# A new order of all operations in a hand-scheduled adaLN, SSM-convolution and gMLP kernel, with four groups of filler matmuls instead of six

## The chip, the core and the metric

The kernel runs on one core of a Trainium2 chip. The metric is the device time in microseconds (us) of that core, the median of several runs. The profile names the engines PE (TensorE matmuls; PEld is its weight load), DVE (VectorE), ACT (ScalarE), POOL (GpSimd) and SP (SyncE, which here only issues DMA transfers).

## What is computed

One transformer-like block on a sequence of 2048 rows of 640 columns, all in bf16, with a condition `c` that gives six row vectors.

```python
mod = silu(c) @ w_mod                                   # six vectors sa, ca, ga, sb, cb, gb of 640
h = layernorm(q) * (1 + ca) + sa
kv = short_conv(k, shift_k) * v                         # four taps along the sequence
y  = irfft(rfft(kv, 2S) * rfft(ssm_k, 2S))[:S] + kv * ssm_D     # long convolution by FFT
x  = q + ga * (h * y)
h = layernorm(x) * (1 + cb) + sb
z = gelu(h @ w_in);  z1, z2 = halves of 864;  z2 = layernorm(z2)
g = w_sp @ z2 + b_sp                                    # w_sp is 2048 x 2048
out = x + gb * ((z1 * g) @ w_out)
```

## The kernel before

**Operations and their order.** The kernel first builds a list of 1438 operations (`Plan.op`). An operation is a small closure that issues one or more instructions: `taps` is 64 matmuls, `csum` one tensor-tensor step, `ldwo` seven DMA transfers. Each has a number, a kind, the letters of the engines that may run it, and the operations that it depends on. Nothing is then decided at run time: the string `ORDER` lists all of them once, each as a letter for its engine (P TensorE, A ScalarE, D VectorE, G GpSimd, S the DMA queue of SyncE) and its number, and `Plan.run` issues them in that order. An engine works through its own tokens one after the other; an instruction that waits for another engine or a transfer holds up all that stand behind it on its engine. So `ORDER` fixes both which engine does a step and what stands in front of what in each queue.

**The convolution** (the first 145 us or so) runs in five units of 128 columns, `u` = 0 to 4. For each, the taps of the short convolution are matmuls against diagonal matrices (`taps`), VectorE multiplies them with `v` (`tv`), a transposing DMA regroups the result (`kvt`, L625), and a first transform stage of matmuls (`s1`, evicted by `s1c`, L272) feeds the second: eight `fwd` matmul groups for the filter (evicted by `khc`) and eight for the signal, whose products are taken on VectorE (`prod`, L489), summed on GpSimd or VectorE (`csum`, L503), transformed back on TensorE (`inv`) and evicted (`zc`). The result is transposed by a DMA (`zt`) or, for the last unit, on TensorE (`zfl`), and multiplied into `gh`, the normalized and modulated input (`ln1`, `xn`, `ghm` at L727). The tables of cosines that all this uses are made at the start on VectorE, GpSimd and ScalarE (`turns` L370, `msub`, `msin`, `msgn`, `mneg`, `gcopy`, `gneg`), and the column `D` is widened (`dwide`), turned and added to the filter (`addD`, L427). `res` adds the branch to `x`.

**The fillers** are matmuls of the identity with itself, 512 columns each, into a PSUM tile that nobody reads. `FILLS` gives the number in each group; the profile shows them as `s<-ident`.

**The gate's input** (about 130 to 205 us) runs in four groups of 512 rows. Statistics (`ln2`, `ag2`, `rstd2`, `nmr2`), normalization (`zx`), a turn into column order (group 0 by TensorE, `hfl`, L928; groups 1 to 3 by a transposing DMA, `turn`, L959), modulation (`hmod`, or `hmod2` at L967, five per group), 16 matmul groups `zz` with GELU behind each, statistics (`stz`, `agz`) and normalization (`zn`) of the second half.

**The mixing and the last product** (from about 180 us) form the 2048 x 2048 product and the output projection by Strassen-like schemes. For each of eight pairs `p` of row blocks, two transposed loads of `w_sp` (`wT`, L1044), four sums (`ssum`, L1057), and seven products `prodw`; VectorE and GpSimd join them with the bias `bcol` and with `z1` into `u` (`c11`, `partial`, `c22a`, `c22b`, `c22m`, `lsa`, and the product step `lsm`, L1115), a transposing DMA turns `u` (`turnu`), sums are formed (`usum`, in the function `u_sum`), and eight products of 320 columns (`pq`, L1291) or the plain form (`pp`, L1304) are joined with `x` (`os`, `oa`, `ox`, `pa`) and stored. `w_out` is loaded by seven transfers (`ldwo`, L1154) and multiplied by `gb` in place (`gbm`, L1159).

Of the kernel before, what the change touches and what calls it, by code (L numbers as in the profile page):

```python
# [33 lines left out]
FILLS = (4, 6, 2, 2, 4, 3, )  # L34
# [9 lines left out]
G5 D13 D101 D0 D14 A1 G102 S525 D103 S2 D116 D15 P7 A10 S23 D104 S83 S84 S26 G122 D117 G6 A4 P1034 A38 S24 D18 A532 P8  # L44
D128 D123 A11 A118 G25 A119 S27 A16 P39 D17 D20 D87 D110 S3 D88 A533 G120 A125 D19 D111 P1033 P146 P41 A124 D40 D42
A147 D105 A21 S524 P1036 P152 G121 A148 A113 P155 A153 A534 P43 G126 P45 D154 D44 A112 D46 G47 G127 A107 A157 P143 G114
A156 D528 P149 P1035 D22 A106 S89 A151 D150 P9 P1037 D144 D91 G115 P164 A535 P228 S85 P174 A165 P162 D108 P134 G56 A229
A12 G109 D529 A176 S86 D530 P183 D135 A163 D531 A175 P234 P137 P177 A184 D138 S28 D179 A185 P172 P140 A235 S526 P230
D141 D178 A173 D29 P180 G136 S30 D182 D536 A231 P166 G142 A181 A167 P48 D32 P168 D539 D540 A169 P158 A159 D49 G139 S31
P232 A233 P160 P170 P52 A161 P248 D53 G537 D538 A171 P186 D187 A541 A249 S527 S566 P54 G554 G188 A542 G131 A550 A543  # L50
D55 P50 D51 G132 P196 P212 P57 D197 G189 P63 G198 P202 D58 P59 D213 D64 P190 P206 G555 G145 G199 D203 A129 A544 D60 P61
P200 G214 P218 S90 A191 D62 P569 A545 D201 A546 S92 G551 G215 D207 D130 P567 G65 P216 D219 P252 S571 A253 P204 A217
P240 S33 P222 A241 P258 P220 G34 D223 G552 A570 D547 P238 P246 A259 P254 A239 S35 A247 D255 P192 A568 P574 P572 D193
P244 G553 P256 D575 S93 P236 A221 D94 G224 D573 G208 S576 A245 A257 P68 A205 D209 G556 S95 G548 P260 A237 G225 P302
A303 D671 P226 D549 P270 D261 P210 G562 P308 D262 D271 P66 A227 A211 P286 A309 A558 G563 G263 P292 G557 P306 P194 D67
D287 P242 D293 A307 P264 P304 G37 A243 G564 A195 P266 P250 D69 G272 A305 P577 D565 A251 P326 D267 G592 D288 D578 A265
A327 P70 P322 D74 D593 P332 A323 P316 G559 D594 D273 D97 D71 D613 P314 P294 A333 G560 P328 D598 A317 P296 P274 A315 S36
G289 P280 A329 S600 G561 A295 D595 D596 P376 A377 D652 D297 P72 P310 A311 G597 P330 D281 D73 A331 P276 G617 A275 P290
P579 D277 P378 A379 D291 P278 A279 G599 G298 P318 P334 D650 P380 G299 D580 S96 P601 D614 A319 G282 A381 P366 D335 D367
P268 P382 A383 P350 P75 G283 P324 A325 D602 P300 D351 P603 P384 D76 P370 D336 G710 A385 P400 A401 D604 G619 D371 P312  # L60
G337 A313 A301 P605 D269 G712 P77 G656 S98 P404 P392 G675 P284 P344 G620 P338 D618 D606 S581 A405 D100 G372 D657 G373
A393 P402 D345 P607 A285 P320 G346 D78 A321 P396 P352 P386 D608 G347 D403 A397 P340 S621 P79 G615 D341 D353 A387 D80
P360 P450 A339 P354 G609 D361 D616 A451 P81 P406 D673 G653 D355 P374 P388 A407 P368 P454 A375 P622 P398 G610 A389 G362
D654 P348 S757 G651 D82 A369 D623 P414 G363 G676 P582 S99 A399 P408 A455 A349 G356 P624 D415 D409 P456 G357 P440 P364
P358 D441 A457 A583 P418 A365 G410 P452 A359 D625 P390 G411 P626 A453 G677 G672 D419 P342 D627 P428 A391 A343 P474 G420
D429 P628 D655 P464 A475 A465 P412 P462 G430 A463 D629 G431 P476 G421 S584 G630 P394 A477 S658 P585 P444 A395 D635 D636
P480 P434 D637 A586 D445 A413 P422 D435 G446 P432 G447 P424 D425 A481 A423 G436 P478 A479 P458 G437 D631 G674 P416 A459
P482 P472 D433 P448 P659 A417 P438 D483 A473 P518 G645 G484 P460 D660 P661 A449 P426 G711 A439 A427 D519 P492 D662 P663
D634 G485 P442 S758 D664 P665 D493 D708 A461 P468 A443 S679 D494 G714 P486 A469 P466 G520 P488 A467 D633 A487 D489 G495
P498 G521 D499 P496 A497 P470 P522 D666 A471 P508 G678 A523 D509 P514 G670 G667 P500 P502 P490 A501 P680 A491 D515 D503  # L70
G510 P516 G511 D681 D504 G505 P682 D683 A517 P512 G713 P506 D513 A507 P684 D685 P716 P686 P718 A717 D632 D687 P722 P720
D719 G668 D721 P724 G709 A723 P725 P727 G688 A133 D689 D690 P726 D728 S587 D729 P750 P736 D731 D730 D760 P588 D759 G693
D732 D639 D733 G761 D762 A763 D735 G764 D737 D738 D695 G703 G715 P1038 P766 D739 D691 P765 A589 D767 D734 D768 D769
# [12 lines left out]
D944 A994 D1002 P1023 A991 G1053 D831 D1049 D995 P1017 D1009 A1024 D923 D1003 D1010 P1011 P957 A1012 G1058 D1063 G1051
A1018 A958 P1013 G961 P1015 D989 P1071 D962 D992 A965 D996 G1027 A1014 A1016 D1064 D963 D1060 D964 D1028 P1025 D966
P945 D1065 A1072 P1073 S1044 D1032 D1030 A1031 A1026 A1029 A946 D1069 A1074 P1075 D1066 P1077 D1076 P1078 D1067 D1068
D1052 D1079 P1019 D1080 D1070 P1083 D1084 P1021 G1081 A1020 P1087 A1022 D1088 P1132 S1082 D1265 G1101 P1125 P1127 D1267
P1137 G1062 D1102 S1092 G1085 D1086 G1089 A1126 P1129 D1133 D1138 A1128 D1139 P1131 P1141 D1134 S1091 D1130 P1152 G1135  # L90
S1094 D1105 P1270 P1145 D1142 P1272 D1103 D1104 A1146 D1271 D1140 S1090 P1149 G1106 P1147 D1153 S1093 P1157 D1143 A1148
D1273 D1158 G1269 D1159 P1151 S1136 S1144 D1150 P1275 G1280 P1161 P1165 D1154 P1172 D1107 A1166 P1177 G1155 P1169 S1097
D1109 P1284 A1285 G1110 D1282 S1274 D1162 S1156 D1170 D1276 D1173 P1277 D1160 G1266 D1268 P1167 P1185 D1178 G1281 D1112
S1095 P1286 P1181 G1163 P1296 A1186 A1287 D1111 S1164 D1278 A1168 P1289 D1108 D1283 P1189 S1096 D1297 G1304 D1290 P1187
G1293 G1292 P1298 D1179 P1171 D1190 D1288 A1188 G1305 P1294 D1182 D1180 D1307 G1291 P1192 D1295 S1098 P1313 P1301 D1299
P1308 D1115 P1191 D1183 D1174 D1193 G1306 A1309 D1302 G1175 D1113 P1310 P1197 S1176 P1205 D1194 D1198 S1279 A1311 D1314
S1184 S1300 P1320 D1312 G1199 P1332 P1207 P1201 D1114 D1117 P1212 G1200 G1317 P1318 P1322 G1195 D1328 G1116 D1202 A1206
P1209 D1321 A1208 D1203 A1333 G1315 S1303 G1329 D1118 P1334 D1319 D1213 P1217 G1316 D1323 P1325 P1344 D1218 P1337 D1326
G1331 D1210 P1211 D1338 S1196 D1345 D1214 D1215 S1204 D1120 S1099 A1335 D1119 D1352 P1225 S1324 D1353 G1219 P1346 P1356
# [54 lines left out]
def kernel(  # L154
# [79 lines left out]
    with ExitStack() as pctx:  # L234
# [25 lines left out]
        op = plan.op  # L260
# [1013 lines left out]
        def u_sum(e, p, k):  # L1274
            if "R" not in T:
# [143 lines left out]
```

## Time and profile before

| What | Value |
|---|---|
| median of 3 runs | 312.57 us (312.31 to 313.37) |
| the profiled execution | 311.67 us |
| its span | 309.9 us |
| TensorE busy | 294.7 us, 95% |
| VectorE busy | 266.3 us, 86% |
| GpSimd busy | 207.3 us, 67% |
| ScalarE busy | 164.0 us, 53% |
| granted clock | 1.00 |

The span is the part of the execution that the profiler recorded between the first and the last instruction. A group row of the profile reads: line, engine, operation, output and input tiles, shape, count, then busy time, mean duration in ns, and the idle time just before them with its releaser. A timeline row reads: start in the span, duration, engine, line, operation, tiles, and in brackets the idle time before it and what ended it.

### The profile page before, as it was taken

The page shows a single profiled execution, that of the slowest core. Times are in us where ns is not written, and L with a number is a line of the kernel's source. Part 1 is how long each engine was busy: PE and PEld are TensorE (multiplying, and loading weights), DVE is VectorE, ACT ScalarE, POOL GpSimd, SP SyncE. Part 2 cuts the span into 40 slices and gives each one's busy share as a digit, 9 for nine tenths or more (in the row PEclk, how much of TensorE's full clock was granted, in tenths as well). Part 3 has the DMA queues.
Part 4 walks back from the last instruction along what each step waited for, and adds up shares of the span by engine and source line. Part 5 has one row for each costly group of instructions (what it writes and reads, how often), then busy time and mean ns, then how long its engine had stood idle before and what let it go on. Part 6 is the DMA issues. An engine that isn't in the chain of part 4 may idle for free.

```text
span 309.9 us, 6954 instructions
## 1 busy us (share of the span) xinstructions
PE 294.7 (95%) x2728; PEld 206.1 (67%) x2728; DVE 266.3 (86%) x510; ACT 164.0 (53%) x301; POOL 207.3 (67%) x225
## 2 busy tenths in 40 slices
PE   5989999999999998899999799999999999999995
PEld 3759989999899887664555355555555555655654
DVE  7998989999999899998795898979965789879584
ACT  8999898886678854657758856511110211020210
POOL 6645878866998988795629924175465729576790
PEclk9999999999999999999999999999999999999999
DMA  8999989979389957005989700037764622583333
GB/s 185 244 156 276 270 221 230 239 162 219 64 214 187 184 142 193 2 2 86 203 133 239 147 2 0 2 44 170 147 150 97 136 66 59 122 147 94 83 77 109
DMA packets 122964, 42.64 MB, mean 138 GB/s; under 512 B 108751, under 2 KB 122932, under 8 KB 122932
## 3 DMA queue, kind: packets, MB, share of 16 engines
q1 hardware_dynamic: 122778, 42.16, 64.5%
q8 instruction: 21, 0.34, 0.5%
q14 instruction: 11, 0.09, 0.1%
q10 hardware_dynamic: 154, 0.05, 0.1%
HBM read 16.11 MB, written 2.62 MB: 60 GB/s over the span
## 4 chain that ended last, share of the span: by engine, by line
PE 66%; DVE 11%; DMA 10%; POOL 8%; SPq 2%; issue 1%; ACT 0%; POOLq 0%; DVEq 0%
PE ps L1082 23%; PE pu L269 11%; PE pz L269 9%; PE sm L269 7%; PE po L1291 6%; PE s L269 4%; DMA big<-in_A_k_dram 4%; DMA ZT<-Z 3%; PE po L1304 2%; DMA Z<-Z 2%; PE pz L1082 2%; DVE st L770 2%; POOL xt L764 1%; PE pu L1082 1%; DMA bsp<-in_B_b_sp_dram 1%
## 5 line engine op out<-in xcount | busy, mean ns | idle before, releaser
L269 PEld LDWEIGHTS <-Z 128*128 128x128 bf16 x320 | 31.1, 98 | 30.0 <-DVE Z L967 2.6
L269 PE MATMUL pu<-X,M 128*128 128x128 bf16 (+1 forms) x480 | 45.8, 237 | 2.5 <-DVE X L272 1.1
L269 PEld LDWEIGHTS <-M 128*128 128x128 bf16 x480 | 37.0, 98 | 6.3 <-issue 2.1
L1082 PEld LDWEIGHTS <-S 128*128 128x128 bf16 x256 | 25.0, 98 | 20.5
L503 POOL TENSOR_TENSOR W<-Tf 128x256 bf16<-128x256 f32 x43 | 32.0, 761 | 8.3 <-PE pz L269 3.6
L269 PE MATMUL pu<-big,Z 128*128 128x432 bf16 x160 | 32.6, 346 | 2.1 <-DVE Z L967 2.1
L272 ACT CAST X<-s 128x1024 bf16<-128x1024 f32 x30 | 30.6, 1020 | 6.8 <-PE s L269 6.6
L489 DVE TENSOR_TENSOR Tf<-pu,KH 128x1024 f32<-128x1024 f32 x25 | 30.3, 1217 | 3.2 <-POOL gh L674 1.2
L269 PE MATMUL pz<-big,Z 128*128 128x432 bf16 x160 | 32.5, 346 | 0.6 <-DVE Z L941 0.6
L1082 PEld LDWEIGHTS <-wT 128*128 128x128 bf16 x192 | 18.8, 98 | 15.5 <-issue 0.2
L1356 ACT COPY O<-po 128x320 f32<-128x320 f32 x12 | 5.0, 427 | 43.4 <-PE po L1291 26.0
L272 ACT CAST KH<-pu 128x512 bf16<-128x512 f32 x40 | 23.4, 596 | 7.8 <-PE pu L269 7.7
L269 PEld LDWEIGHTS <-G 128*128 128x128 bf16 x330 | 24.8, 98 | 2.0 <-ACT Z L272 0.3
L272 ACT CAST Z<-pz 128x512 bf16<-128x512 f32 x34 | 20.1, 598 | 7.4 <-PE pz L269 7.3
L1082 PE MATMUL ps<-X,wT 128*128 128x432 bf16 x112 | 22.7, 346 | 0.0
L1082 PE MATMUL ps<-T,S 128*128 128x432 bf16 x112 | 22.6, 346 | 0.0
L1082 PE MATMUL ps<-X,S 128*128 128x432 bf16 x112 | 22.6, 346 | 0.0
L269 PE MATMUL sm<-dg,big 128*128 128x128 bf16 x320 | 21.6, 224 | 0.4 <-DMA big<-in_A_k_dram 0.4
L269 PEld LDWEIGHTS <-big 128*128 128x128 bf16 x320 | 19.4, 100 | 1.0 <-DMA big<-in_A_k_dram 0.6
L269 PEld LDWEIGHTS <-X 128*128 128x128 bf16 x288 | 17.7, 97 | 3.3 <-DVE X L427 0.9
L996 DVE BATCH_NORM_STATS2 stz<-X 128x6 f32<-128x432 bf16 x32 | 18.0, 591 | 1.8 <-ACT X L990 1.8
L489 DVE TENSOR_TENSOR T<-pu,KH 128x1024 bf16<-128x1024 f32 x15 | 18.1, 1215 | 0.5 <-PE pu L269 0.4
(223 smaller groups left out, 696.6 us busy)
## 6 DMA issues: line engine op xcount, KB each, us to landing
wm<-in_w_mod_dram SPq DMA_DIRECT2D x6, 800.0 KB, 5.2
xt<-in_A_q_dram SPq DMA_DIRECT2D x4, 640.0 KB, 5.6
out_dram<-ot SPq DMA_DIRECT2D x15, 160.0 KB, 2.0
big<-in_B_w_in_dram SPq DMA_DIRECT2D x2, 1080.0 KB, 7.2
X<-in_A_ssm_k_dram SPq DMA_DIRECT2D x4, 512.0 KB, 6.0
ZT<-in_A_v_dram SPq DMA_DIRECT2D x1, 1024.0 KB, 8.2
big<-in_A_v_dram SPq DMA_DIRECT2D x1, 1024.0 KB, 6.8
w_o<-in_B_w_out_dram SPq DMA_DIRECT2D x6, 160.0 KB, 3.5
```

Of the source, the lines that this page charges most:

```text
L269: nc.tensor.matmul(o, lhsT=w, rhs=x, start=start, stop=stop)
L272: (e.copy if e is nc.scalar else e.tensor_copy)(dst, src)
L489: e.tensor_tensor(T_[:], (tl[pu] if src is None else tl[src])[:, :, :, None, :].to_broadcast(shape), tl[KH][:, :, None, :, :].to_broadcast ...
L503: e.tensor_tensor(tl[W][:, :, o, :], T_[:, :, 0, o, :], T_[:, :, 1, 1 - o, :], op=ALU.add if o else ALU.subtract)
L764: op("GD" if u < NU - 1 else "D", "res", lambda e: e.tensor_tensor(sl, sl, gl, op=ALU.add), r=[("gh", (u, g))], w=[("xt", (u, n)) for n in ...
L770: op("D", "ln2", lambda e, n=n: e.bn_stats(out=st2[:, n, (0, 0, 0, 1, 2)[u], :], in_=xt[:, n, us[0] * DU:(u + 1) * DU]), r=[("xt", (v, n)) ...
L996: op("D", "stz", lambda e, i=i, n=n, fc=fc: e.bn_stats(out=stz[:, n, fc, :], in_=tl[z2][:, i, fc * FC:(fc + 1) * FC]), r=[(z2, (i, fc))], ...
L1082: nc.tensor.matmul(ps[:, :FC], lhsT=lhs[:, s_, :], rhs=rhs(s_), start=(s_ == 0 and not more), stop=(s_ == HT - 1), skip_group_check=more)
L1291: nc.tensor.matmul(ps[:, :HS], lhsT=w(k), rhs=x(k), start=start and k == 0, stop=stop and k == n - 1, skip_group_check=True)
L1304: e.matmul(po[t, i][:, :hi - lo], lhsT=uTs[t][:fsz[ft], ft, :], rhs=T["w_o"][:fsz[ft], ft, lo:hi], start=(ft == 0), stop=(ft == NFT - 1))
L1356: late("A", "ok", lambda e: e.copy(rows(i), po[p, b][:, :HS]), r=[o[b]], w=[O[i]], new=[(O[i], "O%d" % i)])
```

## The change

All operations are put into another order, 153 of them on another engine; the number of groups of fillers goes from six to four, with 10 filler matmuls instead of 21; and the expressions of `u_sum` are written otherwise, for the same instructions. As there are two filler operations fewer, each operation with a number above 1036 has in the new string a number lower by two.

```diff
-FILLS = (4, 6, 2, 2, 4, 3, )
+FILLS = (4, 2, 2, 2, )
...
 ORDER = """
-G5 D13 D101 D0 D14 A1 G102 S525 D103 S2 D116 D15 P7 A10 S23 D104 S83 S84 S26 G122 D117 G6 A4 P1034 A38 S24 D18 A532 P8
-D128 D123 A11 A118 G25 A119 S27 A16 P39 D17 D20 D87 D110 S3 D88 A533 G120 A125 D19 D111 P1033 P146 P41 A124 D40 D42
...
+D18 D101 D0 G102 A1 S83 D13 P7 P1033 D103 A10 S2 S23 A38 G47 D15 A4 S26 D14 G5 D110 D116 G6 D104 S84 A16 P8 D25 D117
+P1034 D111 D17 A112 P39 D11 S27 A119 D87 A113 P146 D105 A118 D114 A107 D122 S3 P41 D147 S89 D40 D88 A106 S24 A148 G120
...
-            x, y, o = ((u(hi, 0), u(hi, 1), ALU.add), (R[0], u(lo, 0), ALU.subtract), (u(lo, 0), u(hi, 0), ALU.subtract),
-                       (u(lo, 1), R[1], ALU.subtract))[k]
-            e.tensor_tensor(R[k], x, y, op=o)
+            x = u(hi, 0) if k == 0 else R[0] if k == 1 else u(lo, k - 2)
+            y = u(hi, 1) if k == 0 else u(lo, 0) if k == 1 else u(hi, 0) if k == 2 else R[1]
+            e.tensor_tensor(R[k], x, y, op=ALU.add if k == 0 else ALU.subtract)
```

Tokens that the prediction follows, read off the two strings: on VectorE, the operations ahead of the first product and of the last `tv` of the first unit; `dwide` (G6 in both strings) and the four `turns` (104, 110, 116, 122); the two first `zx`; the five `hmod2` of group 3 (978 to 982), of which the old string gives VectorE two, GpSimd one and ScalarE two, and the new one VectorE two and GpSimd three; `ssum` 1058, from GpSimd to VectorE; several `lsm`, `usum` and `c22b` of the late part, from GpSimd to VectorE. In SyncE's queue the old string has `turn` 1, `bsp`, three `wT`, `turn` 2, a `wT`, the seven `ldwo`, `turn` 3; the new one has `turn` 1, the seven `ldwo`, `bsp`, two `wT`, `turn` 2, `turn` 3, and then more `wT`. At the end, one of the last products of the projection changes places with its neighbour.

More of the change, by code (lines that the diff above doesn't have):

```diff
@@ L49 @@
[L49 to L73, printed above, removed]
@@ new lines @@
+P230 G65 P52 P196 D53 D197 A231 P186 D187 S31 P54 P50 G198 D55 D51 A534 P248 G56 G188 P218 D219 P567 G189 S527 A249
+A568 P202 D203 A535 G199 P569 D536 P57 G537 D58 A570 P190 P212 D213 P61 P200 P192 S90 G214 S571 P59 P222 A191 A543 P252
+A544 A201 A253 D193 G215 D62 P204 P206 D538 P216 A545 G554 D223 G550 P258 D207 P574 A259 D60 P236 S526 S92 A237 D217
+G551 D205 P246 P256 P63 A247 D539 P194 P238 A257 P250 A546 D540 D575 D541 D94 A239 P254 S33 S35 G208 A251 P220 A255
+P240 G224 P244 D34 A241 A245 P302 A303 P242 P572 D555 P260 D64 G552 A243 G209 A195 P306 P66 G225 P276 D542 A307 P308
@@ new lines @@
+D547 D573 P210 D261 P68 A221 G553 A556 D277 G548 S93 D549 D67 A309 P270 P304 D271 P280 A211 G262 P72 S95 G558 A557 G263
+P226 G592 P292 A562 G563 A305 D69 D281 A227 S576 G650 P264 G37 D293 A265 A564 P326 D708 P316 G282 A327 D559 G272 P70
+P266 D97 D73 D594 A565 P278 A317 G273 P376 G283 D267 D598 A377 P294 P286 P332 G714 P310 G560 G74 S36 G619 A333 P577
+D287 P296 P328 D71 D297 A311 D130 A295 A329 P312 D578 A313 P579 D561 P314 D599 D596 P330 D595 P75 A279 A315 D656 A331
+P318 P322 P378 D615 A319 D593 P284 P350 P274 G288 A379 P380 S600 G298 D289 S96 A323 S98 A381 D597 D616 D580 A285 G299
@@ new lines @@
+D835 D695 P778 D837 A786 P779 P813 A789 G669 A783 D782 P817 D836 D612 A814 D780 D781 D707 G839 D698 D840 D841 A784 P792
+D642 D844 A843 D645 D744 D745 G842 D752 D748 D647 P827 A818 D646 P809 A828 S845 D702 A793 P806 D643 D701 G849 S1044
+S1043 S1037 D700 A807 G846 D644 A810 D787 P823 D749 D747 P821 P795 D790 D648 A822 D902 G848 A796 D904 D753 P799 D746
+D699 D903 D641 S1038 D850 A824 P825 A800 P802 D847 A826 D901 D706 P819 P851 A852 D704 G905 P887 D906 A803 A888 D907
+P883 D808 A884 D910 D801 D755 A820 D794 D908 P889 P858 D649 G909 P893 D1053 A859 S911 P865 D811 G1049 P872 D967 A890
@@ new lines @@
+G1048 P875 D756 A894 A866 D913 P868 A876 P854 D970 D853 D705 A873 A869 P879 A912 D754 D969 D870 D812 G916 A855 D968
+P885 D797 D791 G915 A880 A886 P861 D867 P891 G971 A914 P881 D972 G973 A892 A974 D798 D860 A882 D975 P917 A862 D976 A918
+D804 D856 P945 A946 D874 D805 P934 P938 G829 G1046 S977 G981 D857 A935 P920 P927 S1039 G980 D877 D1054 A939 G982 A928
+D878 A921 D863 P924 D1045 D936 D871 A925 D864 D978 P953 P931 D922 D919 D830 A954 P947 G1050 P941 A932 A942 D834 A948
+D979 P990 D1056 D929 G1051 P983 D933 A991 D943 A984 D937 P1000 D940 P986 D944 G895 D1055 D992 A1001 A987 P1004 A1005
@@ L108 @@
+D1253 S1373 D1260 D1261 P1404 G1399 P1395 S1254 A1403 D1396 P1407 G1400 S1262 A1405 G1406 P1412 D1408 P1414 D1409 D1413
+D1401 D1415 P1419 S1397 G1411 P1416 P1422 G1410 D1420 D1417 P1424 D1423 S1421 P1427 D1425 D1428 P1430 S1418 D1431 S1426
+P1433 D1434 S1429 S1435 A1432
 """
```

76 lines of the change are left out of this document (39 added, 37 removed).

## The prediction

> **What bounds the kernel now.** I read the page first, then the windows by stage, the waits of TensorE, and the timeline at the few places where TensorE stands.
>
> ```profile
> span 309.9 us, 6954 instructions
> ...
> PE 294.7 (95%) x2728; PEld 206.1 (67%) x2728; DVE 266.3 (86%) x510; ACT 164.0 (53%) x301; POOL 207.3 (67%) x225
> ...
> PE   5989999999999998899999799999999999999995
> ...
> PEclk9999999999999999999999999999999999999999
> ...
> PE 66%; DVE 11%; DMA 10%; POOL 8%; SPq 2%; issue 1%; ACT 0%; POOLq 0%; DVEq 0%
> ```
>
> TensorE is busy for 294.7 of 309.9 us, and is 66% of the chain that ended last. So 15.2 us is all that any order can win from its idle time, beside work taken off TensorE. The windows say where it lies (columns: TensorE, its weight loads, VectorE, ScalarE, GpSimd, the granted clock, DMA share and rate):
>
> ```profile
> 0.00:35.00 35.00, 29.83 (x324) 23.04 (x325) 31.35 (x86) 31.86 (x69) 20.51 (x37) 1.00 1.06 217
> 35.00:81.00 46.00, 46.00 (x615) 42.62 (x613) 44.12 (x64) 38.98 (x66) 36.83 (x43) 1.00 0.91 205
> 81.00:145.00 64.00, 59.76 (x869) 50.37 (x867) 59.50 (x114) 41.73 (x71) 55.89 (x63) 1.00 0.60 127
> 145.00:176.00 31.00, 31.00 (x172) 16.63 (x170) 23.93 (x69) 23.14 (x44) 19.79 (x22) 1.00 0.94 187
> 176.00:205.00 29.00, 26.86 (x148) 14.15 (x146) 26.73 (x50) 15.36 (x28) 9.70 (x8) 1.00 0.01 1
> 205.00:300.00 95.00, 95.00 (x563) 54.85 (x562) 75.13 (x118) 12.91 (x27) 62.31 (x54) 1.00 0.53 109
> 300.00:310.00 10.00, 6.22 (x52) 4.43 (x49) 5.55 (x12) 0.00 (x0) 2.28 (x3) 1.00 0.49 128
> ```
>
> Idle TensorE: 5.2 us up to 35, none to 81, 4.2 us up to 145, none to 176, 2.1 us in 176 to 205, none to 300, 3.8 us at the end. VectorE is the second bound: it works 31.4 of 35, 44.1 of 46 and 59.5 of 64 us in the first three windows. From 205 on TensorE never stands, so a new order can there only lose.
>
> **The change, part by part.** 153 operations change their engine, and nearly every queue is re-ordered; none is dropped but eleven filler matmuls (21 become 10). All else in the sum is waits. The rewritten tuple of `u_sum` issues the same instructions: nothing.
>
> *The fillers and the start.*
>
> ```profile
> 2.62 2.74 PE L269 MATMUL s<-ident 128*128 128x512 bf16 x6
> ...
> 2.91 0.84 DVE L370 TENSOR_SCALAR T<-KH,mstep 128x256 f32<-128x256 f32 x2
> ...
> 2.99 3.07 POOL L370 TENSOR_SCALAR T<-KH,mstep 128x256 f32<-128x256 f32 x2 [0.67 <-DVE KH L359]
> ...
> 6.27 0.25 PE L269 MATMUL sm<-ident,KH 80*128 80x80 bf16 x1 [0.91 <-POOL big L569]
> ...
> 9.80 0.53 PEld L269 LDWEIGHTS <-X 128*128 128x128 bf16 x4 [0.70 <-DVE X L427]
> ...
> 15.35 3.24 SPq L625 DMA_TRANSPOSE X<-Z  x2
> ...
> 16.19 1.02 PE L269 MATMUL s<-ident 128*128 128x512 bf16 x4
> ...
> 18.28 0.60 PE L269 MATMUL pu<-X,M 128*128 128x256 bf16 x6 [1.07 <-DVE X L272]
> ...
> 19.45 0.33 PEld L269 LDWEIGHTS <-X 128*128 128x128 bf16 x4 [0.19 <-DMA X<-Z]
> ...
> 31.23 1.22 DVE L489 TENSOR_TENSOR Tf<-pu,KH 128x1024 f32<-128x1024 f32 x1
> ```
>
> At 16.19 four fillers take 1.02 us, so eleven are some 2.8 us of TensorE work. But the work behind the fillers waits anyway: at 6.27 for GpSimd, at 9.80 for VectorE's `addD` (its weight load idled 0.70), at 18.28 for a VectorE copy (1.07 idle after the last early filler). Taken out, they leave these waits where they were. I book 0, with the bound of 2.8 us below. What covers them is VectorE's queue; if it came earlier they would have cost up to that.
>
> What moves the start is that queue. Up to the first product (31.23) 48 VectorE steps stand in front now, 47 in the new order: steps such as `ln1f` and table copies, 8.2 us by their rows in the timeline, go behind it, and 6.1 us come in (two `turns` of GpSimd, three copies, two negations, one row of statistics): 2.1 us less. One GpSimd step of 3.07 us (`turns`, 0.84 for the same on VectorE) no longer stands ahead of `dwide`, so the first taps can start near 5.3 instead of 6.4. Against it: the last of the four `tv` of the first group has 2.9 us more VectorE work in front of it (32 steps, not 24), and the transposed load behind it (15.35 here, used at 19.45, 4.1 us later) comes late by as much. Bounds -2.1 and +2.9 us; both are paid only in part, since ScalarE's `s1c` copies lie between. Their own queue loses four statistics rows ahead of that point and gains copies (+1.0 us). I take -0.6: the queue in front of the product is the one that TensorE's saturated stretch hangs on.
>
> TensorE's own rate is the other price of few fillers: six of them take 2.74 us at 2.62, 0.46 each, and four 1.02 at 16.19, 0.26 each, while the granted clock is written as full in all windows. So TensorE starts at half rate here and had left it by 16. The Trainium skill ("TensorE: Matmul & The Clock Gate", Part 1) has a rule that speaks against this change: the array starts at half clock and is let up only after a window of about 3.4 us of sustained work, and falls back after an idle one. The trace agrees with the half rate at the start (0.46 against 0.26 us); no run here shows a fall back. It is the third rival below, priced there from rows.
>
> *35 to 145.* VectorE's load ahead of the last product of the convolution hardly changes: by the means of like steps 19.9 us leave and 20.7 come, +0.8. GpSimd gets 9 us lighter in this stretch. Examples of what is exchanged:
>
> ```profile
> L727 DVE TENSOR_TENSOR gh<-gh,gca_bf 128x512 bf16<-128x512 bf16 x10 | 5.0, 513 | 0.0
> ...
> L727 POOL TENSOR_TENSOR gh<-gh,gca_bf 128x512 bf16<-128x512 bf16 x10 | 11.8, 1193 | 0.0
> ...
> L1115 POOL TENSOR_TENSOR u<-c,G 128x432 bf16<-128x432 f32 x4 | 4.6, 1160 | 0.2
> ...
> L1115 DVE TENSOR_TENSOR u<-c,G 128x432 bf16<-128x432 f32 x4 | 3.3, 834 | 0.0
> ...
> PE sm L928 <- ACT Z L913: 1.1, 1, 1.1
> ```
>
> TensorE's 4.2 idle us here are many small waits, the longest 1.1 us (`hfl` waiting on `zx`). The wait for `zx` stays: its chain (statistics, GpSimd's `rstd`, `zx`) is the same in the new order, with the two `zx` only exchanging engines. The others are of pairs of queues that arrive a few tenths apart, and the products now come in another order with three `csum` fewer on VectorE in front of the last. Bounds: -4.2 (all gone), +2.1 (one wait as long as the longest that VectorE causes later, 2.14 at 176, below). I take -1.3, the small ones without `zx`, by half.
>
> *The wait at 176.*
>
> ```profile
> 141.69 3.07 SPq L959 DMA_TRANSPOSE Z<-Z  x1
> ...
> 145.43 7.38 SPq L1044 DMA_TRANSPOSE wT<-in_B_w_sp_dram  x3
> ...
> 155.75 3.56 SPq L959 DMA_TRANSPOSE Z<-Z  x1
> ...
> 161.39 3.75 SPq L1154 DMA_DIRECT2D w_o<-in_B_w_out_dram  x7
> ...
> 171.94 0.75 DVE L967 TENSOR_SCALAR Z<-Z,cb_col,sb_col 128x512 bf16<-128x512 bf16 x1 [0.68 <-PE pz L269]
> ...
> 174.76 1.51 POOL L1159 TENSOR_TENSOR w_o<-w_o,gb_bf 96x640 bf16<-96x640 bf16 x1
> 174.95 3.56 DVE L967 TENSOR_SCALAR Z<-Z,cb_col,sb_col 128x512 bf16<-128x512 bf16 x1
> ...
> 176.24 2.11 POOL L1057 TENSOR_TENSOR S<-wT,S 128x1024 bf16<-128x1024 bf16 x1
> ...
> 178.57 0.72 PE L269 MATMUL pu<-big,Z 128*128 128x432 bf16 x3 [2.14 <-DVE Z L967]
> ```
>
> TensorE waits 2.14 us for the last `hmod2` of group 3, which took 3.56 us on VectorE, where its twin at 171.94 took 0.75; GpSimd ran two tensor-tensor steps beside it. In the new order `ssum` 1058 (the one of 2.11 us) goes to VectorE behind both, three of the group's five `hmod2` run on GpSimd and two on VectorE, and the queue of SP has `turn` of group 3 directly behind that of group 2, no longer behind a `wT` load and the seven `w_o` loads (3.75 us). Those now stand ahead of `turn` of group 2: 3.75, two `wT` of 2.46 (7.38 / 3) and an estimated 0.5 for the short load of `bsp`, 9.2 us from the end of `turn` 1 (141.69 + 3.07 = 144.8), that is to 154.0, and that `turn` was issued at 155.75 because its rows were not ready: covered, by 1.8 us. VectorE's work ahead of the last `hmod2` is the same within 0.6 us, but TensorE has 4.2 us less in front of that point (prefix of the queue, fillers included), so it comes sooner. So the wait does not vanish by order alone; it shrinks by the 2.8 us that the long step loses and grows by TensorE's earlier coming. I take -1.5; bounds -2.1 and +2.1 (a second step stretched as this one was).
>
> The Trainium skill ("GPSIMD Engine Reference", 1. Specifications) says that GpSimd's memory interface is shared with VectorE, and that instructions of VectorE in a two-port mode contend. The trace agrees with its direction: 3.56 us beside GpSimd's steps against 0.75. By that rule two `gbm` of GpSimd, which stand around the new place, would stretch these steps again, and the term would be nearer -0.5; by the twin's row it is -1.5.
>
> *205 to 300.* VectorE takes on some 9 us here (lsm, usum, c22b by the means of both engines), onto 75.1 of 95; GpSimd loses 15 of 62.3. TensorE has no idle time, so the term is 0 to +2.9 (half an `lsm` of 0.834 us late in each of seven pairs); I take 0.
>
> *The end.*
>
> ```profile
> 300.74 1.11 DVE L1344 TENSOR_TENSOR O<-O 128x320 f32<-128x320 f32 x1
> ...
> 302.49 0.70 PE L1291 MATMUL po<-V,uT 128*128 128x320 bf16 x4 [0.81 <-DVE ot L1350]
> ...
> 303.03 4.00 PE L1304 MATMUL po<-w_o,uT 128*128 128x320 bf16 x35
> ...
> 307.07 0.33 DVE L1310 TENSOR_TENSOR ot<-po,xt 128x160 bf16<-128x160 f32 x1 [0.16 <-PE po L1304]
> ```
>
> The product at 302.49 waits 0.81 us for VectorE; the new order puts it ahead of the product that now fills part of that wait (four matmuls, 0.5 us), and the VectorE step of 1.11 us still stands in front. +0.3 (bounds -0.8, +0.8).
>
> Sum: 0 - 0.6 - 1.3 - 1.5 + 0 + 0.3 = -3.1 us. The profiled execution took 311.67 us (span 309.9 and 1.8 around it), 0.9 below the median of the three runs, 312.57. So 308.6 for a profiled execution, and 309.5 for the median.
>
> **Rivals.** First, slower: VectorE is the bound from 205 on. Place: the evictions of TensorE's banks (`lsa`, `c22a`, `pa`), which stand in VectorE's queue behind `usum` and `lsm` taken from GpSimd (0.834 us for one `lsm`). For it: VectorE works 75.1 of 95 us and gets 9 more; in the page's slices TensorE has no gap that would absorb a late one. Against it: GpSimd's share falls by 15 us, and steps such as the 3.56 us one show what its company costs. Price: one `lsm` late in each of eight pairs, 8 x 0.83 = 6.6 us, less the 3.1: +3.5, 316.1. It decides from four late ones.
>
> Second, no change: VectorE's queue sets the first 145 us, and its work is the same (+0.8); the small waits go elsewhere, the two terms -0.6 and -1.3 are 0 and the wait at 176 shrinks by 0.5: 312.57 - 0.5 + 0.3 = 312.4.
>
> Third, TensorE stays at half rate beyond 10 us for want of fillers. Some 5 us of matmuls stand between 10 and 18; at half rate they need 10 in a stretch of 8 us, so 2 us are lost: 311.5. Against it: the waits of this stretch are VectorE's.
>
> **How the numbers follow.** Forecast 0.55; slower 0.20; no change 0.15; half rate 0.10. Within 0.3% is 0.94 us, about what a measurement of this kernel can tell from no change. Slower by more: 0.20. Same: 0.12 of the second and 0.02 of the third, 0.14. Faster: 0.55, 0.03 and 0.08: 0.66. The range runs from 305.5 (the first three terms at -2.1, -4.2 and -2.1 with TensorE still meeting 1.3 of new waits) to 314.0, part of the way into the slower case. The forecast's own range is 306.5 to 311.5.
>
> **What would show it.** Right: TensorE idle under 3.5 us in the window where 4.2 stands now, no 3.56 us `hmod2`, the wait at 176 below 1 us, and still no idle from 205 to 300. The start is right if VectorE's first product begins before 30.5. Wrong: gaps of 0.3 to 0.8 us on TensorE from 205 on released by VectorE (first rival); filler-like rates of 0.43 us for 512 columns past 12 us (third); a wait for `Z<-Z` before group 2, if the `w_o` loads delay that `turn`.

## The result and the profile after

The new order takes 309.13 us in the median of 18 runs (307.48 to 311.97), the old one 312.67 (310.48 to 316.35) in runs beside it: ratio 0.9899, 95% interval 0.9869 to 0.9929, so about 1% faster. Two repeats on other chips (e1, e11 below) give 0.9922 and 0.9909. The forecast was 309.5, between 305.5 and 314.0.

The profiled execution of the new kernel is the slowest of its 18: 311.97 us, with a span of 310.2, longer than the 309.9 of the old kernel's profile. It has to be read together with a second profile. First its page (the granted clock is the last row):

```profile
span 310.2 us, 6932 instructions
...
PE 292.4 (94%) x2717; PEld 204.7 (66%) x2717; DVE 268.6 (87%) x544; ACT 161.4 (52%) x292; POOL 175.8 (57%) x197
...
PEclk9999999999999999999997999999999999999999
```

The windows of the same execution, with the columns as before:

```profile
...
35.00:81.00 46.00, 44.26 (x590) 40.82 (x588) 42.22 (x72) 41.76 (x69) 35.29 (x41) 1.00 0.95 202
81.00:145.00 64.00, 60.51 (x877) 50.96 (x876) 61.85 (x123) 43.66 (x75) 50.19 (x57) 1.00 0.58 133
145.00:176.00 31.00, 28.42 (x148) 14.77 (x146) 22.57 (x64) 16.83 (x33) 15.95 (x20) 0.94 0.66 133
176.00:205.00 29.00, 29.00 (x161) 15.54 (x160) 26.80 (x58) 16.51 (x30) 9.28 (x10) 1.00 0.26 50
205.00:300.00 95.00, 95.00 (x562) 54.78 (x561) 77.99 (x132) 12.90 (x27) 46.56 (x38) 1.00 0.49 108
300.00:310.20 10.20, 6.53 (x53) 4.53 (x50) 5.76 (x14) 0.00 (x0) 2.81 (x3) 1.00 0.47 125
```

And the windows of the same kernel in a second execution (308.3 us, span 306.5, the first experiment below):

```profile
...
35.00:81.00 46.00, 43.57 (x582) 40.16 (x580) 42.04 (x71) 41.22 (x68) 34.66 (x41) 1.00 1.03 204
81.00:145.00 64.00, 60.52 (x883) 51.28 (x881) 61.49 (x121) 43.77 (x74) 50.61 (x57) 1.00 0.57 130
145.00:176.00 31.00, 31.00 (x172) 16.62 (x170) 24.95 (x70) 19.27 (x38) 19.30 (x21) 1.00 0.78 152
176.00:205.00 29.00, 29.00 (x161) 15.54 (x160) 25.96 (x58) 15.05 (x26) 8.54 (x10) 1.00 0.28 53
205.00:300.00 95.00, 94.19 (x561) 54.59 (x560) 79.16 (x136) 12.38 (x26) 47.20 (x38) 1.00 0.50 109
```

Three things are to be seen. The 2.1 us of idle TensorE in 176 to 205 are gone in both. The stretch 35 to 81, where TensorE never stood, now has 1.7 to 2.4 us of idle time. And 145 to 176, full in the old kernel and in the second execution, has 2.6 us of idle time in the first one, with the granted clock at 0.94.

That last stretch is where the two executions part. On ScalarE of the first one:

```profile
161.13 0.81 ACT L965 ACTIVATE Z<-Z,sb_col,cb_col 128x512 bf16<-128x512 bf16 x1 [3.47 <-DMA Z<-Z]
```

On TensorE:

```profile
158.75 1.08 PE L269 MATMUL pz<-big,Z 128*128 128x432 bf16 x5
162.41 1.07 PE L269 MATMUL pz<-big,Z 128*128 128x432 bf16 x5 [2.58 <-ACT X L990]
...
164.80 2.01 PE L269 MATMUL pz<-big,Z 128*128 128x432 bf16 x5
```

In windows of 2 us behind that:

```profile
162.00:164.00 2.00, 1.59 (x8) 0.83 (x8) 2.00 (x10) 1.90 (x4) 1.21 (x4) 0.91 0.00 0
164.00:166.00 2.00, 2.00 (x7) 0.88 (x6) 1.64 (x6) 0.96 (x2) 1.70 (x2) 0.50 0.00 0
166.00:168.00 2.00, 2.00 (x10) 0.95 (x9) 2.00 (x5) 1.39 (x4) 0.04 (x1) 0.74 0.01 4
```

ScalarE comes to the first `hmod2` of group 2 at 157.7, and its rows, turned by a DMA, are not there until 161.13. Behind that step in ScalarE's queue stand GELU steps of group 1, whose data were ready; they would have emptied TensorE's banks. So TensorE waits 2.58 us for a transfer that its next product doesn't need. Then the granted clock is 0.5: five matmuls that take 1.07 us take 2.01. The missing clock in the three windows, 2 x (0.09 + 0.50 + 0.26), is 1.7 us. Together 4.3 us, and the first profile stands 3.7 us behind the second at its end (its start had been 0.7 ahead).

The SyncE queue shows part of why the rows come late (`w_o` loads, then two `wT`, then `turn` 2 and 3):

```profile
142.77 3.37 SPq L1154 DMA_DIRECT2D w_o<-in_B_w_out_dram  x7
146.19 0.43 SPq L1143 DMA_DIRECT2D bsp<-in_B_b_sp_dram  x1
146.66 7.52 SPq L1044 DMA_TRANSPOSE wT<-in_B_w_sp_dram  x2
...
154.36 16.09 SPq L959 DMA_TRANSPOSE Z<-Z  x2
```

The rows were written by 153.25, and `turn` 2 is issued at 154.36, behind two `wT` whose issue took 3.76 us each in the mean (4.55 and 2.91) where 2.46 had been reckoned. It lands 6.8 us later. In the second execution the same queue issues it at 154.05, it lands in 5.0, and TensorE doesn't wait at all:

```profile
154.05 14.15 SPq L959 DMA_TRANSPOSE Z<-Z  x2
...
159.05 0.81 ACT L965 ACTIVATE Z<-Z,sb_col,cb_col 128x512 bf16<-128x512 bf16 x1 [0.66 <-DMA Z<-Z]
```

So of the 2.8 us by which ScalarE waits longer in the first execution (3.47 for 0.66), 0.3 are the later issue, 1.8 the longer time to landing and 0.7 ScalarE's earlier arrival. What makes the landing slower in one execution than in the other is not shown.

### The profile page after: what moved, and what is told of

It reads as the page before. It is cut to its first block, busy times and chain, and to the rows that moved or that the text cites. A ratio compares the mean times of both kernels' runs of the same rounds, so it can differ in the third digit from the quotient of the medians.

```text
span 310.2 us, 6932 instructions
## 1 busy us (share of the span) xinstructions
PE 292.4 (94%) x2717; PEld 204.7 (66%) x2717; DVE 268.6 (87%) x544; ACT 161.4 (52%) x292; POOL 175.8 (57%) x197
## 4 chain that ended last, share of the span: by engine, by line
PE 54%; DVE 10%; SPq 5%; POOL 4%; DMA 2%; issue 2%; ACT 1%; DVEq 0%; POOLq 0%; ACTq 0%
PE ps L1082 23%; PE pu L269 9%; PE pz L269 8%; PE po L1291 6%; PE po L1304 2%; SPq L1044 2%; DMA Z<-Z 2%; DVE Tf L489 2%; PE pz L1082 2%; POOL W L503 2%; PE sm L269 2%; PE s L269 2%; PE pu L1082 1%; DVE st L770 1%; DVE T L489 1%
## 5 line engine op out<-in xcount | busy, mean ns | idle before, releaser
L503 POOL TENSOR_TENSOR W<-Tf 128x256 bf16<-128x256 f32 x46 | 33.9, 754 | 13.2 <-DVE Tf L489 4.4
L269 PE MATMUL pz<-big,Z 128*128 128x432 bf16 x160 | 33.8, 353 | 2.6 <-ACT X L990 2.6
L272 ACT CAST X<-s 128x1024 bf16<-128x1024 f32 x31 | 31.7, 1022 | 4.4 <-PE s L269 4.3
L272 ACT CAST Z<-pz 128x512 bf16<-128x512 f32 x36 | 21.1, 600 | 4.9 <-PE pz L269 4.6
L1090 ACT ACTIVATE m<-ps,bcol 128x432 f32<-128x432 f32 x7 | 4.4, 624 | 28.6 <-PE ps L1082 17.4
```

The lines of the kernel that those rows point to most:

```text
L269: nc.tensor.matmul(o, lhsT=w, rhs=x, start=start, stop=stop)
L272: (e.copy if e is nc.scalar else e.tensor_copy)(dst, src)
L503: e.tensor_tensor(tl[W][:, :, o, :], T_[:, :, 0, o, :], T_[:, :, 1, 1 - o, :], op=ALU.add if o else ALU.subtract)
L1090: e.activation(part[p, m][:], part[p, BANK[m]][:, :FC], ACT.Identity, bias=T["bcol"][:, p + HT:p + HT + 1], scale=1.0)
```

## The experiments

All in one table first: medians against runs of the old kernel on the same chip. The runs of one group shared their chip; between groups only the ratios are to be compared.

| Kernel | us | old kernel | ratio (95%) |
|---|---|---|---|
| e1 new, again | 308.61 | 311.30 | 0.9922 (0.9903 to 0.9941) |
| e2 new, GELU first | 309.75 | 311.30 | 0.9938 (0.9916 to 0.9960) |
| e3 new, `w_o` later | 316.22 | 311.30 | 1.0161 (1.0133 to 1.0190) |
| e4 old, 6 fillers | 319.19 | 311.30 | 1.0256 (1.0235 to 1.0276) |
| e5 new, 21 fillers | 309.76 | 310.93 | 0.9968 (0.9955 to 0.9982) |
| e6 old, one `hmod2` moved | 309.72 | 310.93 | 0.9967 (0.9954 to 0.9979) |
| e7 new, then old | 314.02 | 310.93 | 1.0101 (1.0076 to 1.0126) |
| e8 old, then new | 311.50 | 310.93 | 1.0030 (1.0012 to 1.0048) |
| e11 new, again | 308.80 | 311.42 | 0.9909 (0.9874 to 0.9943) |
| e9 new, `turn` 2 earlier | 308.66 | 311.42 | 0.9904 (0.9872 to 0.9935) |
| e10 old, GpSimd away | 310.23 | 311.42 | 0.9953 (0.9932 to 0.9975) |
| e12 new, 6 fillers | 308.45 | 311.32 | 0.9899 (0.9848 to 0.9951) |

**e1 and e11: the new kernel again.** No edit.

> The changed kernel once more, for a second profile. In its first profile ScalarE stood 3.47 us at the first `hmod2` of group 2, waiting for the transposed rows, with three GELU steps of group 1 behind it; TensorE waited 2.58 us for those, and the granted clock was then 0.5 for some 3.4 us. Theory A: this wait is in the order and comes back in every execution with a length that varies; a wait about as long is followed by the low clock and a span near 310, a clearly shorter one is not, and leaves a span of 306 to 308. Theory B: the low clock is an accident of that execution; it comes without such a wait or the wait comes without it. Ratio to the kernel before 0.987 to 0.993 by both.

> The new kernel unchanged, as the reference of the two beside it on the same chip, and for a third profile: ratio to the old kernel 0.987 to 0.994. If the wait at the first `hmod2` of group 2 on ScalarE is long (2.5 us on TensorE) the low clock stands behind it, if it is short (under 1 us) it does not.

The wait varies as theory A has it: none in e1 (span 306.5), 1.94 us in e11 (span 309.9), 2.58 in the first profile, and only behind the last does the low clock stand. Of the 31 runs of the unchanged new kernel whose clock is listed, two have a mean clock of 0.994, and they are the slowest two of their 18. A span of 309.9 without the low clock was not expected: beside the 1.94 us, e11 comes 0.9 us later than e1 to the end of the convolution (124.76 for 123.89, at the step shown in the section on the prediction) and waits 0.47 us more at 177.

**e2: ScalarE's order.** `A912` moved behind `A886`.

```diff
-... A912 ... A855 ... A880 ... A886
+... A855 ... A880 ... A886 A912
```

> One step moved: the `hmod2` of group 2 stands on ScalarE behind the three GELU steps, not ahead of them. Theory A (head of the line on ScalarE): TensorE goes on with three more products (2.7 us) while the rows land; the wait there falls from 2.6 to at most 0.7 us, the clock stays at 1.00, and the time is 1.5 to 2.5 us under e1_again. Theory B (the rows are late anyway, TensorE waits for them a product later): within 0.6 us of e1_again.

Nearest to theory B: no gain (0.9938 beside 0.9922; by the medians 1.1 us over e1, more than that theory allows). In its profile the rows land at 160.67, and the GELU steps and TensorE pass without a wait. But VectorE has an `hmod2` of the same rows ahead of the statistics of group 3, and GpSimd two ahead of its `rstd2`; on ScalarE a `zx` (974) waits for these, with the next GELU behind it:

```profile
164.68 0.92 ACT L914 ACTIVATE Z<-xt,nmr,rstd 128x640 bf16<-128x640 bf16 x1 [2.08 <-issue]
```

TensorE waits 1.57 us for that GELU at 166, and 0.9 later on. To let one queue pass doesn't help while another stands behind the same rows.

**e3: the `w_o` loads later.** `S1044` moved behind `S911`.

```diff
-S845 S1044 S1043 S1037 S1038 S911 S977
+S845 S1043 S1037 S1038 S911 S1044 S977
```

> The seven `w_o` loads (3.4 us of SyncE's queue) stand behind `turn` 2 and no longer ahead of `bsp`, two `wT` and `turn` 2. Theory A (those loads and the `wT` behind them delay `turn` 2): it is issued when its rows are there, near 153.3 instead of 154.36, lands a microsecond or more earlier, and the wait of 2.6 us shrinks by 1 to 2; time 0.7 to 1.8 us under e1_again. Theory B (the loads are covered, as the prediction had it: the last row came at 153.25): within 0.5 us of e1_again.

Neither: 4.9 us slower than the old kernel. `turn` 2 is indeed issued at 153.02 and its rows are used from 158.01 on, but GpSimd's queue has two `gbm` ahead of two `hmod2`, and they need the loads. GpSimd:

```profile
162.50 2.75 POOL L1160 TENSOR_TENSOR w_o<-w_o,gb_bf 128x640 bf16<-128x640 bf16 x2 [11.35 <-DMA w_o<-in_B_w_out_dram]
165.23 1.52 POOL L968 TENSOR_SCALAR Z<-Z,cb_col,sb_col 128x512 bf16<-128x512 bf16 x2
```

TensorE:

```profile
166.81 1.45 PE L270 MATMUL pu<-big,Z 128*128 128x432 bf16 x7 [2.95 <-POOL Z L968]
```

So the early place of these loads belongs to the early place of their readers. A transfer can't be moved alone.

**e4: the old order with six fillers.**

```diff
-FILLS = (4, 6, 2, 2, 4, 3, )
+FILLS = (1, 1, 1, 1, 1, 1, )
```

> The old order with one filler matmul in each of its six groups, 6 instead of 21: fifteen fewer, 3.9 us of TensorE at 0.26 us each. Theory A (booked in the prediction: they lie in waits that remain): within 0.9 us of the kernel before. Theory B (the fillers stand on the path): 2 to 4 us less, which would be most of the change's whole gain. Theory C (fewer fillers keep TensorE at half rate longer): some 2 us more, with 0.43 us and more for 512 columns past 12 us.

Theory C at the start, and more behind it. TensorE:

```profile
10.63 1.91 PE L269 MATMUL sm<-dg,big 128*128 128x128 bf16 x16
...
14.47 2.01 PE L269 MATMUL sm<-dg,big 128*128 128x128 bf16 x32
183.46 3.78 PE L269 MATMUL pu<-big,Z 128*128 128x432 bf16 x10 [3.96 <-DVE Z L967]
```

Sixteen taps take 1.91 us at 10.6 and 32 of them 2.01 at 14.5: full rate comes at some 14.5, not 16.4 as the text on e12 has it; the old kernel has it from 10.2 on. TensorE is 2.0 us late at 126. Those 2 us then became 7.4 at 190, in a place that has nothing to do with fillers: VectorE and GpSimd come together at another moment. VectorE:

```profile
177.75 3.65 DVE L1013 TENSOR_SCALAR X<-X,mvz,rstdz 128x864 bf16<-128x864 bf16 x1
```

A normalization step that takes 0.49 us took 3.65 beside GpSimd's `gbm` and `ssum`, the last `hmod2` behind it was late, TensorE waited 3.96 us, and the clock was low for about 6.8 us, twice as long as in the first profile of the new kernel:

```profile
180.00:184.00 4.00, 0.54 (x2) 0.28 (x3) 3.92 (x5) 1.24 (x2) 2.64 (x2) 0.73 0.26 58
184.00:188.00 4.00, 4.00 (x13) 1.67 (x11) 3.65 (x8) 1.23 (x3) 0.00 (x0) 0.50 0.00 0
188.00:192.00 4.00, 4.00 (x21) 2.06 (x20) 1.33 (x4) 3.04 (x6) 0.00 (x0) 0.92 0.00 0
```

**e5 and e12: more and fewer fillers in the new order.** `FILLS = (8, 4, 4, 5, )` and `FILLS = (1, 1, 2, 2, )` in place of `(4, 2, 2, 2, )`.

> The new order with 21 filler matmuls again, as many as before, in its four groups (8, 4, 4, 5). TensorE's idle time is 15.2 us in the profile of the old kernel and 15.2 in e1_again, so the whole gain could be the eleven fillers. Theory A (the gain is the fillers' own time): 2.5 to 3.5 us over the new kernel, no faster than the old one. Theory B (fillers stand in waits, and the new order needs fewer because its matmuls follow each other more closely): at most 1.2 us over the new kernel.

> The new order with one filler matmul instead of four and of two in its first two groups; TensorE is then less busy between 2.8 and 5.7 us. Theory A (what the fillers buy is the full rate, which the new kernel has from 8.0 us, the old one from 10.2, and the old order with six fillers from 16.4): full rate comes later than 10 us, the first product of VectorE starts 0.5 us or more later than 28.4, and the time is 0.5 to 2.5 us over the new kernel (ratio to the old one 0.993 to 1.000). Theory B (at the start the fillers only fill waits): within 0.4 us of the new kernel (0.989 to 0.992).

Four fewer at the start change nothing that can be measured (0.9899, theory B; span 306.3 for the 306.5 of e1), though full rate does come later, as theory A has it. TensorE of e12:

```profile
8.91 1.68 PE L269 MATMUL sm<-dg,big 128*128 128x128 bf16 x16
...
16.32 1.04 PE L269 MATMUL pu<-X,M 128*128 128x256 bf16 x12
```

TensorE of e1 at the same steps:

```profile
8.56 1.06 PE L269 MATMUL sm<-dg,big 128*128 128x128 bf16 x16
...
16.30 1.04 PE L269 MATMUL pu<-X,M 128*128 128x256 bf16 x12 [0.68 <-ACT X L272]
```

Full rate comes some 2 us later, the taps take 1.68 us for 1.06, and the step behind them begins at the same time, since the steps on the way wait for ScalarE (0.68 us at 16.30 in e1, 0.66 at 12.19 and 0.61 at 14.94 in e12). With eleven more fillers (e5) the ratio is 0.005 to 0.007 above those of e1, e11 and e12 on other chips, 1.4 to 2.1 us, between the two theories. Its profile shows no cost at the fillers: the first product of the second transform stage begins at 16.25 (16.30 in e1), the convolution's last transposes at 123.70 (123.89). Its span is 1.4 us over that of e1, and two waits of TensorE at 161 and 175 make that up, 0.82 and 0.62 us; e11 has the same two with few fillers (1.94 and 0.47). No unchanged new kernel ran on the chip of e5, so whether its slower median is due to the fillers stays open.

**e6: one step moved in the old order.** `D978` moved behind `D979`.

```diff
-G895 D979 G980 A981 D830 D1050 D832 ... D896 ... D897 P934 D978
+G895 D979 D978 G980 A981 D830 D1050 D832 ... D896 ... D897 P934
```

> The old order with one step moved: on VectorE the last `hmod2` of group 3 (978) stands directly behind the other one (979), ahead of two `nmrz`, a `gbm` and two `zn`, and so not beside GpSimd's two tensor-tensor steps. Theory A (the prediction's third term, the 2.14 us at 176): the step takes 0.4 to 0.8 us, the wait at 176 is gone, and the time is 1.5 to 2.3 us under the old kernel. Theory B (something else is late next): within 0.7 us of it.

Half of theory A: the wait at 176 is gone, TensorE gains 2.3 us there against the old kernel's profile, and gives 0.8 back by the products of pair 0 (TensorE stands 0.4 us between 186 and 205, where it stood for nothing). The median is 1.2 us lower.

**e10: GpSimd away from that step.** `G1053`, `G1058` and `G1051` become `D1053`, `D1058` and `D1051` behind `D833`; 978 keeps its place.

> The old order, with the `hmod2` of group 3 that took 3.56 us (978) left where it is, and the three tensor-tensor steps that GpSimd ran at 174.8, 176.2 and 178.3 (two `gbm`, one `ssum`) given to VectorE, behind it. Theory A (GpSimd's company is what stretches the step): it takes 0.4 to 0.8 us, the wait at 176 falls under 0.5, and the time is 0.8 to 2 us under the old kernel, as with the step moved. Theory B (it is stretched by something else, or stands too late by its place): it takes over 2 us again, and the time stays within 0.5 us.

Theory A. VectorE:

```profile
174.76 0.40 DVE L968 TENSOR_SCALAR Z<-Z,cb_col,sb_col 128x512 bf16<-128x512 bf16 x1
```

The same step in the same place takes 0.40 us for 3.56, the wait at 176 is gone, and the median falls by 1.2 us. So it was GpSimd's company and not the step's place in the queue. The ends of the rows agree: in the old kernel the step ended at 178.51, 0.2 us behind the second of GpSimd's two steps (176.24 and 2.11), and the stretched step of e4 ended 0.2 us behind the second one beside it.

**e7 and e8: halves of both orders.** New up to 132 us and old behind, and the reverse, joined where the first `zz` starts.

> The new order up to about 132 us (start, convolution, with its three early fillers), the old one behind it. Theory A (two separate gains, some 1 us up to the first `zz` and some 2.3 us at 176): 0.7 to 1.6 us under the old kernel, with the wait at 176 of 1.5 us or more still there. Theory B (the start's gain is what matters): 2.5 us or more under. Theory C (an earlier arrival is given back at 176, where the rows of group 3 do not come earlier): within 0.5 us of the old kernel.

> The reverse: the old order with its five early groups of fillers up to about 133 us, the new one behind it. Theory A: the wait at 176 is gone, 1.5 to 2.8 us under the old kernel. Theory B (the gain is at the start): within 0.7 us of the old kernel.

e7 misses every theory. e8 lies 0.6 us over the old kernel, inside the range of theory B, but not for its reason: the wait at 176 shrinks to 0.54 us, as theory A has it, and the gain is lost elsewhere. Between the convolution's end and the ninth `zz`, where they are joined, e7 loses 2.6 us and e8 1.8 against the old kernel; statistics steps that one order does earlier and the other later fall together there, and the clock is low behind it (0.50 in e7 from 132 to 138). So the two tell nothing on the two gains: an order can't be cut there.

**e9: `turn` 2 earlier in the new order.**

```diff
-D910 D801 D755 D794 D908 D649 D1053 D811 ... D867
+D910 D908 D801 D755 D794 D649 D811 ... D867 D1053
-S1037 S1038 S911 S977
+S1037 S911 S1038 S977
```

> The new order with three steps moved, so that `turn` 2 starts earlier: the last `zx` of group 2 (908) stands two statistics steps earlier on VectorE, `turn` 2 stands ahead of the second `wT` in SyncE's queue, and the `ssum` that needs that `wT` stands behind the next statistics of VectorE. Theory A (the late rows of group 2 are what makes the new kernel vary): `turn` 2 is issued near 152 instead of 154, its rows land before ScalarE comes to them, no wait on a product of group 1 behind them, no low clock in any execution; median 0.4 to 1.5 us under the new kernel. Theory B (the rows land as late as before, since the transfers share their engines with `wT`): within 0.4 us of the new kernel.

The mechanism goes the way of theory A, the time is as in theory B. `turn` 2 is issued at 153.21 (154.05 in e1; theory A had 152), lands in 5.4 us, and ScalarE doesn't wait for its rows:

```profile
158.72 0.81 ACT L966 ACTIVATE Z<-Z,sb_col,cb_col 128x512 bf16<-128x512 bf16 x1
```

No wait of TensorE is left there, but e1 had none either. Its six runs lie between 308.46 and 309.32, those of the unchanged kernel beside them between 308.21 and 311.72; the medians differ by 0.14 us, which is nothing. That it takes away the long waits is suggested by the narrower range of six runs and not shown; the median is not lower. No version tried here is measurably faster than the new kernel.

## Why the prediction came out right, step by step

The sum was right, its parts less so. Against the old kernel's profile (span 309.9), the second profile of the new one (306.5, no late rows) shows where the 3.4 us lie:

| Term | forecast | shown by the two profiles |
|---|---|---|
| fillers | 0 | 0 at the start (e12); for all eleven not settled (e5) |
| start | -0.6 | -0.2 for start and convolution together |
| 35 to 145 | -1.3 | -1.1, all of it behind the convolution |
| wait at 176 | -1.5 | -2.4 |
| 205 to 300 | 0 | 0 |
| end | +0.3 | +0.3 (+0.1 in e11 and e12) |

That the sum came so close is in part luck: the two terms before the wait were booked 0.6 us too large together, and the wait 0.9 too small. And only a part is shown by an experiment: without the wait at 176 the old order gains 1.2 us in the median (e6, e10). The rest is read off the two profiles, and e7 and e8, which were to separate it, could not.

**The start** was right in direction and wrong in what it is worth. VectorE's first product begins early, as forecast (before 30.5). VectorE of e1:

```profile
28.39 2.35 DVE L489 TENSOR_TENSOR Tf<-pu,KH 128x1024 f32<-128x1024 f32 x2
```

But the 2.8 us are given back before the convolution ends. TensorE of e1, three of the waits that the old kernel has not, and the first transposes of the last unit:

```profile
38.96 0.61 PE L269 MATMUL s<-F1ng,X 128*128 128x256 bf16 x4 [0.71 <-DMA X<-Z]
...
64.74 0.60 PE L269 MATMUL pu<-X,M 128*128 128x256 bf16 x6 [0.50 <-DVE Tf L489]
...
73.08 1.05 PE L269 MATMUL sm<-dg,big 128*128 128x128 bf16 x16 [0.89 <-DVE gsa_bf L717]
...
123.89 0.62 PE L787 MATMUL pu<-ident,Z 128*128 128x128 bf16 x8 [0.45 <-ACT Z L272]
```

TensorE of the old kernel at that last step:

```profile
124.07 0.62 PE L787 MATMUL pu<-ident,Z 128*128 128x128 bf16 x8 [0.45 <-ACT Z L272]
```

It comes at 123.1 to 124.8 in the seven profiles that have the new order and its fillers up to there (the first, e1, e2, e3, e7, e9, e11; mean 123.9) and at 122.8 to 124.4 in the four of old order and old fillers (before, e6, e8, e10; mean 123.9). So the convolution gains nothing. VectorE works 135.0 us of the first 145 in the old kernel's profile and 134.7 in that of e1, the same work, as the prediction had reckoned (+0.8) and then not believed; that this is the reason is argued, not tested. The step that failed is "the queue in front of the product is the one that TensorE's saturated stretch hangs on". The second rival was right up to here.

**35 to 145.** The gain is real, in another place: from that step to the ninth `zz` it is 18.42, 18.42 and 18.43 us in the old kernel's profile, e6 and e10, and 17.35 to 17.37 in the first profile of the new, e1 and e11. The sign named for the term came (3.5 us of idle TensorE in the window of 4.2), but the prediction took the small waits by half and left out that for `zx`, and it is the stretch around `zx` that got shorter. TensorE of e1:

```profile
131.46 0.51 PE L928 MATMUL s<-ident,Z 128*128 128x128 bf16 x6 [0.75 <-POOL Z L915]
...
136.11 0.51 PE L928 MATMUL s<-ident,Z 128*128 128x128 bf16 x6 [0.26 <-POOL Z L915]
```

The wait for `zx` is 0.75 instead of 1.1, the second piece comes 2.4 us earlier, a wait of 0.55 at 142 is gone, and one filler fewer stands there.

**The wait at 176** went entirely, where -1.5 of -2.14 was booked. TensorE comes 1.3 us earlier to that point, and the rows of group 3 do too, which the prediction had held against the gain. The last two `hmod2` of VectorE in e1:

```profile
170.33 0.41 DVE L967 TENSOR_SCALAR Z<-Z,cb_col,sb_col 128x512 bf16<-128x512 bf16 x1 [0.41 <-DMA Z<-Z]
...
172.40 0.78 DVE L967 TENSOR_SCALAR Z<-Z,cb_col,sb_col 128x512 bf16<-128x512 bf16 x1
```

No step of 3.56 us is left. e10 settles the mechanism: the same step without GpSimd beside it is 0.40. The sentence of the Trainium skill ("GPSIMD Engine Reference", 1. Specifications) that the two engines share a memory interface agrees with it; that GpSimd's `gbm` would stretch these steps in the new order too, and leave only -0.5, did not come. GpSimd's company stretched another step instead: the `ssum` that moved to VectorE (1058 in the old string) takes 1.87 us in e1, where a `gbm` of GpSimd begins at 173.00, and 0.68 in e10 without one. VectorE of e1, then of e10:

```profile
173.10 1.87 DVE L1057 TENSOR_TENSOR S<-wT,S 128x1024 bf16<-128x1024 bf16 x1
```

```profile
178.88 0.68 DVE L1058 TENSOR_TENSOR S<-wT,S 128x1024 bf16<-128x1024 bf16 x1
```

It stands behind the last `hmod2`, and TensorE does not wait for it.

**The cover over `turn` 2** is the step that was wrong against the new kernel: "covered, by 1.8 us". It reckoned 2.46 us for each `wT`; they took up to 4.55 to issue, the rows of group 2 were ready 2.3 us earlier than in the old order (153.25 for 155.54), and so the queue and not the rows set the start, 1.1 us after the rows. That alone doesn't make the wait: TensorE's wait goes with the time from issue to landing, none at 5.0 us (e1), 0.82 at 6.0 (e5), 1.94 at 7.1 (e11) and 2.58 at 6.8 (the first profile), and what makes that vary stays open. What the wait costs in the two profiles of the unchanged kernel that have it is 1.9 and 2.6 us on TensorE, 4.3 with the clock behind the longer one. The prediction named the sign to look for (a wait for `Z<-Z` before group 2) and gave it no price.

**205 to 300** held: TensorE idles 0 and 0.81 us there, with 3 to 4 us more work on VectorE (77.99 and 79.16 for 75.13), not 9. The first rival did not come. **The end**: the 0.81 is the wait of the old kernel, now split and a little earlier. TensorE of e1:

```profile
296.99 0.57 PE L1291 MATMUL po<-V,R 128*128 128x320 bf16 x3 [0.49 <-DVE ot L1350]
...
298.56 0.70 PE L1291 MATMUL po<-V,uT 128*128 128x320 bf16 x4 [0.32 <-DVE ot L1350]
```

**The third rival**, half rate for want of fillers, did not come in the new order, where even e12 with its later full rate loses nothing, and would have come in the old: e4 has it, 2 us as priced. The new order reaches full rate at 8.0 us with six fillers that lie close together, the old one at 10.2 with ten.

## What to carry to other kernels

A transfer's wait belongs to the queue behind it: put the steps that read a DMA's result behind the work that could go on without it, on every engine that reads it (e2, which did so on ScalarE alone, gained nothing), and ask of each load that is moved ahead of another what its own issue takes when the queue is full. A step can take several times its twin's time because of what another engine runs beside it (3.56 us for 0.40 here), so look for such a step before reading its place in the queue as the cause. An early start is worth only what the bound behind it lets through; find the point at which both versions have done the same work, and compare there.

## What the runs showed of the hardware

TensorE's clock falls again in mid-kernel, each time for 1.7 us of lost clock or twice that. Between 160 and 185 us it went to 0.50 behind waits of 2.58 (the first profile), 2.95 with 1.52 (e3) and 3.96 us (e4), and not behind waits of 1.94 (e11) and 2.14 (the old kernel). At about 130 us, where TensorE has had a stretch of narrow matmuls (16 to 64 columns, 126 to 129), it fell behind waits of 2.04 (e8) and 1.45 us (e7), and in e10 with no wait over 0.5 us in front:

```profile
130.00:132.00 2.00, 1.80 (x8) 0.51 (x7) 1.64 (x6) 1.17 (x2) 1.64 (x3) 0.50 0.00 0
```

The old kernel's profile has the same matmuls there, a wait of 1.09 us, and no fall. So the length of one wait doesn't decide it alone, and no run here isolates what does. The Trainium skill ("TensorE: Matmul & The Clock Gate", Part 1) gives one idle window of about 3.4 us for it. The length of the low stretch agrees (1.7 us lost at half rate is 3.4 us); the waits that it came behind are mostly shorter here.

The mean clock of a run tells how often it came: 0.994 or 0.995 once, 0.989 twice. Of the 74 runs of the old kernel beside the experiments, 21 had it at least once, of the new kernel's 31 two. It does not always cost time. The twelve old runs at 0.994 took 310.2 to 311.3 us, no longer than their neighbours at full clock; the nine at 0.995 or 0.989 took 313.0 to 314.1, some 2 us longer. The profile of e10 (0.994) shows how a low stretch can cost nothing: TensorE needs 18.43 us from the convolution's last transposes to the ninth `zz`, as at full clock, since the waits there shrink (for `zx` 0.20 us for 1.09, at 142 0.39 for 0.55). Whether the other runs at 0.994 are of this kind is not shown.
